# Moving the last gelu into the PSUM evacuation, and the closing spatial pass's partial sum from TensorE to VectorE

## The chip, the cores and the metric

The kernel runs on one core of one Trainium2 chip. The metric is the device time of one execution in microseconds (us). Executions of one kernel spread by several us (the kernel before: 1929.6 to 1937.5), so times here are medians of three to seven executions. Readings inside a run (stage lengths, idle times) come from one profiled execution each. Engines: PE is TensorE (PEld its weight loads), ACT is ScalarE, DVE is VectorE, POOL is GpSimd, SP issues most DMAs. PSUM holds the products that PE writes (`ps_all` in the profiles), SBUF the other tiles. The granted clock is the share of its full clock that TensorE got, by the profile. An "exp" is one instruction of the softmax on ACT, from PSUM to the tile `Pa`.

## The reference, cut to what matters

```python
x = A_x                                        # 1 x 2048 x 512, bf16
for layer in (0, 1):                           # the same weights twice
    n = layernorm(x)
    x = x + attention(n)                       # 32 query heads of 16, one key/value head
    n = layernorm(x)
    z = gelu_tanh(n @ w_in)                    # 2048 x 1792
    z1, z2 = z[:, :896], layernorm(z[:, 896:])
    g = w_sp @ z2 + b_sp                       # "spatial": mixes tokens
    x = x + (z1 * g) @ w_out
```

The spatial product needs z2 of all 2048 tokens, and layer 1's attention needs keys of all tokens of x. So each layer ends with work that few exps can cover.

## The kernel before: the parts that matter

The kernel contains its own planner. Every operation is given a modelled duration, dependencies and a priority. The planner plays the program through with these numbers, and the order in which operations are taken becomes each engine's fixed program order. An operation may list alternative engines (`alts`).

Attention goes in chunks of 512, 512, 512, 256, 128 and 128 tokens. After each chunk its tokens pass through the mixer's first half. The spatial product is done in four passes over the source tiles: 0 to 7, 8 to 11, 12 and 13 (partial sums in fp16 in `gp`), and the closing pass over tiles 14 and 15. `tc` counts eight pairs of target token tiles.

```python
# mixer_chunk, for every chunk: copy out of PSUM (DVE, or ACT as alternative), then gelu in place on ACT
def gl(e):
    e.activation(z1v[:, :, 0:n], z1v[:, :, 0:n], ACTF.Gelu_apprx_tanh)
    return e.activation(z2f[...], z2f[...], ACTF.Gelu_apprx_tanh)
ge = sc.op("act", gl, ..., z1 + z2, -1.0, table="gelu")
...                                   # bn_stats of z2 on DVE after ge, rstd on POOL, normalise on DVE

# spatial(..., final=True), for each tc: 4 PSUM jobs of up to 2 x 256 columns
if final:
    todo.append(("g", None))          # partial sum through an fp16 identity, on PE
todo += [("w", w) for w in ws]        # the two source tiles
...
fn=lambda e, b, ...: e.tensor_tensor(self.hT[...], PSUM, z1r[...], ALU.mult)    # DVE, from PSUM
...                                   # then 2 x 7 output products of 512 columns on PE, priority pr - 0.3,
                                      # and X = PSUM + X on DVE for each of the two tiles
```

`hT` has two buffers, used by turns. Layer 0's closing pass also builds layer 1's keys, pair by pair.

The softmax here doesn't subtract the row's maximum and nothing guards it: scores larger than these inputs give would overflow.

## Time and profile before

1933.8 us, median of three runs (1931.3 to 1937.45). I mark two times in every profile: the end of layer 0's last exp (T0) and the end of layer 1's last exp (T1).

| before | us |
|---|---|
| T0 | 905.2 |
| T0 to T1 (layer 0's end, then layer 1's attention) | 956.7 |
| T1 to the end of the span (layer 1's end) | 71.3 |
| exp work done in the first 200 us after T0 | 124.9 |
| ACT idle from T0 + 200 to T1 | 24.2 |

The view of the exps' line gives 126.2 for the fourth row, since it counts with them a table load of 1.28 us at the same line (timeline, ACT):

```profile
954.28 1.28 ACT L1257 ACT_TABLE_LOAD   x1
```

Over the whole span the busy line of the page has ACT at 90% and DVE at 92%, but at the layers' ends another engine rules. The windows view of the kernel before, three stretches of 10 us from T0 (columns: window, length, busy time and count of PE, PEld, DVE, ACT and POOL, granted clock, DMA share, GB/s):

```profile
905.20:915.20 10.00, 9.30 (x91) 6.87 (x91) 9.95 (x22) 0.60 (x1) 0.77 (x2) 1.00 0.01 2
915.20:925.20 10.00, 7.60 (x75) 5.90 (x74) 8.71 (x17) 5.85 (x8) 0.00 (x0) 1.00 0.07 20
925.20:935.20 10.00, 8.05 (x39) 4.89 (x40) 4.75 (x10) 0.00 (x0) 0.78 (x2) 0.66 0.18 49
```

PE falls idle, and in the third stretch the granted clock is 0.66. The timeline of PE shows why (start, length, engine, line, operation, shapes, count, and in brackets the idle time before it with its releaser):

```profile
919.56 3.44 PE L1034 MATMUL ps_all<-wsT,z2n 128*128 128x256 bf16 x30
927.15 0.40 PE L1032 MATMUL ps_all<-gp,ident_3 128*128 128x256 f16 x1 [4.15 <-DVE z2n L943]
927.34 0.63 PE L1034 MATMUL ps_all<-z2n 128*128 128x256 bf16 x2
```

The closing pass waits 4.15 us for the last chunk's normalised z2 and then runs slowly. In layer 1 the same chunk goes through these steps (timeline, ACT and DVE):

```profile
1877.36 1.28 ACT L921 ACT_TABLE_LOAD   x1
1878.66 0.95 ACT L921 ACTIVATE E<-E 128x896 bf16<-128x896 bf16 x1
1879.51 0.93 ACT L922 ACTIVATE z2n<-z2n 128x896 bf16<-128x896 bf16 x1
...
1880.84 1.14 DVE L934 BATCH_NORM_STATS2 st_18<-z2n 128x6 f32<-128x448 bf16 x2
```

In the last stage PE never rests. The chain of waits (start, length, what):

```profile
1889.46 3.02 PE ps_all L1087 x14
1892.48 0.22 PE ps_all L1034 x2
1892.70 0.11 PE ps_all L1032
...
1894.78 3.02 PE ps_all L1087 x14
```

A pair of token tiles takes 1894.78 - 1889.46 = 5.32 us, of which L1032, the identity product, takes 7 x 0.11.

### The profile page before, as it was taken

How to read it: one execution, taken by the hardware profiler on the slowest of the kernel's cores; microseconds unless marked ns; L12 is line 12 of the kernel's file. 1: busy time of each engine (PE TensorE's matmuls, PEld its weight loads, DVE VectorE, ACT ScalarE, POOL GpSimd, SP SyncE). 2: the span in 40 equal slices, each digit the busy share in tenths (PEclk: the TensorE clock that was granted, in tenths of full speed). 3: DMA queues.
4: the chain of work that ended last, by engine and by line, in shares of the span. 5: the costliest groups of instructions: out<-in, count | busy, mean ns of one | idle time of the engine just before them, and what ended most of it. 6: DMA issues, size and time to landing. Idle time of an engine off the chain costs nothing.

```text
span 1933.2 us, 41389 instructions
## 1 busy us (share of the span) xinstructions
PE 1649.2 (85%) x17431; PEld 671.0 (35%) x17431; DVE 1777.4 (92%) x3198; ACT 1747.3 (90%) x1526; POOL 59.7 (3%) x106
## 2 busy tenths in 40 slices
PE   6777887787989998889987877877788999888899
PEld 3222222122234443555542222222122444335565
DVE  7999999999998898987769999989999899999976
ACT  7999999999999999997379999999999999999960
POOL 3000000000000000000000000000000000000000
PEclk9999999999999999999999999999998999989999
DMA  9700001000001000112100000010000100010123
GB/s 262 191 1 1 1 1 42 1 1 1 1 31 34 23 8 26 46 28 62 53 10 1 1 1 1 1 42 1 1 1 20 34 23 23 2 53 8 29 71 101
DMA packets 96985, 59.84 MB, mean 31 GB/s; under 512 B 39704, under 2 KB 92704, under 8 KB 96800
## 3 DMA queue, kind: packets, MB, share of 16 engines
q1 hardware_dynamic: 95216, 56.64, 10.6%
q8 instruction: 138, 2.26, 0.5%
q10 hardware_dynamic: 1584, 0.56, 0.1%
q14 instruction: 47, 0.39, 0.1%
HBM read 30.97 MB, written 17.83 MB: 25 GB/s over the span
## 4 chain that ended last, share of the span: by engine, by line
ACT 32%; PE 30%; DVE 25%; issue 12%; POOL 1%; ACTq 0%; POOLq 0%
ACT Pa L1257 29%; PE ps_all L1034 8%; PE ps_all L1540 7%; DVE E L1437 5%; PE ps_all L1333 4%; DVE Pd L1475 4%; PE ps_all L1087 3%; DVE E L1473 2%; DVE E L1464 2%; DVE E L1470 2%; DVE gp L1050 2%; PE ps_all L1523 1%; PE ps_all L748 1%; DVE E L1467 1%; ACT z2n L922 1%
## 5 line engine op out<-in xcount | busy, mean ns | idle before, releaser
L1257 ACT ACTIVATE Pa<-ps_all 128x1536 bf16<-128x1536 f32 (+1 forms) x1435 | 1640.0, 1349 | 59.6 <-PE ps_all L1540 46.0
L1540 PE MATMUL ps_all<-qs,kT 32*128 32x512 bf16 (+2 forms) x6144 | 572.8, 315 | 227.9 <-ACT Pa L1257 213.9
L1540 PEld LDWEIGHTS ps_all<-qs,kT 32*128 32x128 bf16 x6144 | 172.6, 92 | 710.1 <-ACT Pa L1257 631.0
L1437 DVE TENSOR_SCALAR E<-ps_all 128x512 int32<-128x512 f32 x510 | 347.9, 685 | 26.8 <-PE ps_all L1540 24.0
L1333 PE MATMUL ps_all<-Pa,V 128*32 128x512 bf16 (+2 forms) x5407 | 331.4, 316 | 2.0 <-DVE oT L771 1.5
L1475 DVE SCALAR_TENSOR_TENSOR Pd<-E 128x1024 uint16<-128x1024 int32 x255 | 310.2, 1217 | 0.8
L1523 PE MATMUL ps_all<-wo_r,zero 128*128 128x512 bf16 (+2 forms) x967 | 257.2, 369 | 2.2 <-DVE E L1437 1.8
L1034 PE MATMUL ps_all<-wsT,z2n 128*128 128x256 bf16 x1456 | 216.8, 276 | 4.7 <-DVE gp L1050 2.9
L1333 PE MATMUL ps_all<-Pd,V 128*32 128x512 bf16 (+2 forms) x737 | 181.0, 324 | 0.0
L1470 DVE TENSOR_TENSOR E<-E 128x1024 f16<-128x1024 f16 x255 | 174.8, 685 | 3.2
L1473 DVE TENSOR_TENSOR E<-E 128x1024 f16<-128x1024 f16 x255 | 174.4, 684 | 2.1
L1464 DVE TENSOR_SCALAR E<-E 128x1024 f16<-128x1024 uint16 x255 | 174.6, 686 | 1.1
L1034 PEld LDWEIGHTS ps_all<-wsT,z2n 128*128 128x128 bf16 x1456 | 119.5, 98 | 72.3 <-issue 36.3
L1333 PEld LDWEIGHTS ps_all<-Pa,V 128*32 128x32 bf16 x5407 | 98.7, 96 | 120.9 <-issue 99.6
L1523 PEld LDWEIGHTS ps_all<-wo_r,zero 128*128 128x128 bf16 x967 | 74.4, 100 | 122.0 <-issue 90.5
L1467 DVE TENSOR_SCALAR E<-E 128x1024 f16<-128x1024 f16 x255 | 106.9, 419 | 2.5
L1466 DVE TENSOR_SCALAR E<-E 128x1024 f16<-128x1024 f16 x255 | 107.0, 420 | 2.2
L1050 DVE TENSOR_TENSOR gp<-ps_all,gp 128x512 f16<-128x512 f32 (+1 forms) x128 | 75.3, 616 | 16.6 <-PE ps_all L1034 16.4
L748 PE MATMUL ps_all<-xnTA,wq_pad 128*128 128x512 bf16 (+2 forms) x384 | 68.8, 312 | 2.7 <-DVE E L1437 2.3
L876 PE MATMUL ps_all<-w_in_r,xnTB 128*128 128x448 bf16 x256 | 64.6, 361 | 1.3 <-DVE z2n L885 0.6
L902 PE MATMUL ps_all<-xnTB,w_in_r 128*128 128x512 bf16 (+2 forms) x336 | 63.0, 310 | 1.7 <-DVE z1s L911 1.4
L771 DVE CAST oT<-ps_all 128x512 bf16<-128x512 f32 (+2 forms) x96 | 48.7, 508 | 7.8 <-PE ps_all L1333 7.3
(79 smaller groups left out, 1168.5 us busy)
## 6 DMA issues: line engine op xcount, KB each, us to landing
wsT<-wsT_scratch SPq DMA_DIRECT2D x18, 512.0 KB, 3.9
wsT_scratch<-gp SPq DMA_DIRECT2D x16, 512.0 KB, 3.7
z1s<-z_scratch SPq DMA_DIRECT2D x16, 448.0 KB, 3.7
z_scratch<-z1s SPq DMA_DIRECT2D x6, 896.0 KB, 4.5
wsT<-wsT_scratch SPq DMA_DIRECT2D x16, 256.0 KB, 2.9
X<-in_A_x_dram SPq DMA_DIRECT2D x8, 256.0 KB, 6.4
z2n<-wsT_scratch SPq DMA_DIRECT2D x2, 1024.0 KB, 7.6
out_dram<-X SPq DMA_DIRECT2D x16, 128.0 KB, 1.7
```

Of the source, the lines that this page charges most:

```text
L1034: ins = e.matmul(o_, self.z2n[:, w[0], f * 128:(f + 1) * 128], w[1], start=st, stop=sp_)
L1050: return e.tensor_tensor(dst, src, dst, ALU.add)
L1257: return e.activation(k.Pa[:, base:base + n, :], k.b32(b0, n).rearrange("p (k q) -> p k q", k=n), ACTF.Exp, scale=SCALE)
L1333: ins = e.matmul(k.b32(k.pvb)[32 * j:32 * j + 32, 0:n], k.V[:, kt, 32 * j:32 * j + 32], b.slot[:, s * n:(s + 1) * n], tile_position=(0, 32 ...
L1437: return k.sc.op("dve", lambda e: e.tensor_scalar(k.eI[:, s, 512 * i:512 * (i + 1)], k.b32(j.bank.idx)[:, 0:512], C_LOG2, C_BIAS, op0=ALU. ...
L1464: return lambda e: e.tensor_scalar(out, a, m, None, op0=ALU.mult)
L1467: return lambda e: e.tensor_scalar(out, a, m, b, op0=ALU.mult, op1=ALU.add)
L1470: o4 = sc.op("dve", lambda e: e.tensor_tensor(q, u, w, ALU.mult), d_sb(n, 0.521e-3), [o3], pr)
L1473: o6 = sc.op("dve", lambda e: e.tensor_tensor(q, q, u, ALU.mult), d_sb(n, 0.521e-3), [o5], pr)
L1475: o7 = sc.op("dve", lambda e: e.scalar_tensor_tensor(po.bitcast(U16), I, 2.0 ** -9, q, op0=ALU.mult, op1=ALU.add), d_sb(n, 1.042e-3), [o6] ...
L1523: ins = e.matmul(k.b32(k.pvb if b is None else b.idx)[:, 0:n], k.zero[:], k.wo_r[:, 0, 0:n], start=b is not None, stop=b is not None)
L1540: ins = e.matmul(self.b32(bank)[:, s * n:(s + 1) * n], self.kT[32 * j:32 * j + 32, kt * 128:(kt + 1) * 128], self.qs[32 * j:32 * j + 32, g ...
```

## The change

Its intent: take 56 identity products per layer off PE, by adding the partial sum on DVE from SBUF, where an fp16 add of 1024 columns took 0.685 us in this profile, as long as a multiply of 512 from PSUM (0.682), and by letting the idle ACT empty PSUM. And bring the last chunk's z2 sooner, by doing the gelu while emptying PSUM, with its table loaded ahead. The core of the diff:

```diff
+GPL = 0                      # identity product only in layers below GPL: nowhere
+MERGE = 9                    # merging of two chunks: never, there are six
@@ mixer_chunk
+con = dict(fn=lambda e, b, cp=cp: e.activation(*cp(b), ACTF.Gelu_apprx_tanh), eng="act", table="gelu", ...)
-   [dict(fn=lambda e, b, cp=cp: e.tensor_copy(*cp(b)), ...)]
+   [con] if last else [dict(fn=lambda e, b, cp=cp: e.tensor_copy(*cp(b)), ...)]
+if last:
+    gs = z2
+    pre = sc.op("act", lambda e: e.activation(self.tiny[:], self.mhalf[:], ACTF.Exp), ..., table="exp")
@@ spatial
-if final:
+if gp_pe:                    # gp_pe = final and layer < GPL
     todo.append(("g", None))
-fn=lambda e, b, ...: e.tensor_tensor(self.hT[...], PSUM, z1r[...], ALU.mult)
+h16 = h_.bitcast(FP16)       # h_ is the slice of hT
+fn=lambda e, b, cp=cp: e.tensor_copy(*cp(b)), dur=d_psum(256 * m), prio=1.1, deps=self.hT_read[par],
+alts=[("act", lambda e, b, cp=cp: e.activation(*cp(b), ACTF.Copy), d_act(256 * m))]
+ad = sc.op("dve", ... tensor_tensor(h16, h16, self.gp[:, tc, f0:f0 + m, :], ALU.add) ...)
+ev = sc.op("dve", ... tensor_tensor(h_, h16, z1r[:, par, f0:f0 + m, :], ALU.mult) ...)
@@ ExpStream.commit, after a layer's last exp
+k.sc.op("act", lambda e: e.activation(k.tiny[:], k.mhalf[:], ACTF.Gelu_apprx_tanh), ..., table="gelu")
# cut: the rewriting of the loads of the third pass, which with these constants gives the same loads
```

More of the change, by code (lines that the diff above doesn't have):

```diff
@@ L289, in job @@
             o = self.op(c.get("eng", "dve"), (lambda en, f=c["fn"]: f(en, j.bank.idx)), c["dur"],
-                        [prev] + outs[-1:] + list(c.get("deps", ())), c["prio"], job=j, alts=alts)
+                        [prev] + outs[-1:] + list(c.get("deps", ())), c["prio"], job=j, alts=alts,
+                        table=c.get("table"))
             outs.append(o)
@@ L418, in __init__ @@
         self.s_fin = 14
+        self.merge = MERGE
         self.ring = [(0, 3), (3, 2)]
@@ L431, in __init__ @@
         self.mhalf = sb([P, 1], FP32, "mhalf")
+        self.tiny = sb([P, 1], FP32, "tiny")
         self.X = sb([P, self.NT, D], BF16, "X")
@@ L882, in cp @@
                     return self.z2n[:, t, h * 448:(h + 1) * 448], self.b32(b)[:, 0:448]
+                con = dict(fn=lambda e, b, cp=cp: e.activation(*cp(b), ACTF.Gelu_apprx_tanh), eng="act", table="gelu",
+                           dur=d_act(448), prio=pr - 1, deps=list(self.z2_read.get(t, ())))
                 pl, (ev,) = sc.job([((lambda e, b, pe=pe: pe(e, b, (0, 1))), 2 * d_mm(448)),
                                     ((lambda e, b, pe=pe: pe(e, b, (2, 3))), 2 * d_mm(448))],
-                                   [dict(fn=lambda e, b, cp=cp: e.tensor_copy(*cp(b)), dur=d_psum(448), prio=pr - 1,
+                                   [con] if last else [dict(fn=lambda e, b, cp=cp: e.tensor_copy(*cp(b)), dur=d_psum(448), prio=pr - 1,
                                          deps=list(self.z2_read.get(t, ())),
@@ L891, in mixer_chunk @@
                 self.xnTB_read.append(pl)
-        z1v = self.z1L if last else self.z1s[:].rearrange("p (f t) -> p f t", f=NF)
+        c0 = g.t0 % 512 if g.ci == self.merge + 1 else 0
+        z1v = (self.z1L if last else self.z1s[:].rearrange("p (f t) -> p f t", f=NF))[:, :, c0:c0 + n]
         z1_war = list(self.dx_s.end) if last else list(self.z1s_free)
@@ L906, in cp @@
             def cp(b, f0=f0, m=len(fs)):
-                return (z1v[:, f0:f0 + m, 0:n], self.b32(b)[:, 0:m * n].rearrange("p (f t) -> p f t", f=m))
+                return (z1v[:, f0:f0 + m, :], self.b32(b)[:, 0:m * n].rearrange("p (f t) -> p f t", f=m))
             w = max(2, 1024 // n)
+            con = dict(fn=lambda e, b, cp=cp: e.activation(*cp(b), ACTF.Gelu_apprx_tanh), eng="act", table="gelu",
+                       dur=d_act(n * len(fs)), prio=pr - 0.9, deps=z1_war)
             pl, (ev,) = sc.job([((lambda e, b, part=mm[i:i + w], pe=pe: pe(e, b, part)), len(mm[i:i + w]) * d_mm(n))
                                 for i in range(0, len(mm), w)],
-                               [dict(fn=lambda e, b, cp=cp: e.tensor_copy(*cp(b)), dur=d_psum(n * len(fs)), prio=pr - 1,
+                               [con] if last else [dict(fn=lambda e, b, cp=cp: e.tensor_copy(*cp(b)), dur=d_psum(n * len(fs)), prio=pr - 1,
                                      deps=z1_war,
@@ L917, in mixer_chunk @@
             self.xnTB_read.append(pl)
+        if g.ci == self.merge:
+            self.held = (T, z1, z2)
+            return
+        t0 = T[0]
+        if g.ci == self.merge + 1:
+            T, z1, z2 = [a + b for a, b in zip(self.held, (T, z1, z2))]
+            t0, T = T[0], T
+            z1v = self.z1s[:].rearrange("p (f t) -> p f t", f=NF)[:, :, 0:128 * len(T)]
+        nt = len(T)
         z2f = self.z2n[:].rearrange("p t f -> p (t f)")
         def gl(e):
-            e.activation(z1v[:, :, 0:n], z1v[:, :, 0:n], ACTF.Gelu_apprx_tanh)
-            return e.activation(z2f[:, T[0] * FH:(T[0] + nt) * FH], z2f[:, T[0] * FH:(T[0] + nt) * FH],
-                                ACTF.Gelu_apprx_tanh)
-        ge = sc.op("act", gl, d_act(NF * n) + d_act(nt * FH), z1 + z2, -1.0, table="gelu")
-        sp = self.dma(lambda e: e.dma_start(self.z1_dv[:, :, g.t0:g.t0 + n], z1v[:, :, 0:n]), [ge],
-                      f"z1s{g.layer}{g.ci}", n * P * NF * 2)
+            e.activation(z1v, z1v, ACTF.Gelu_apprx_tanh)
+            return e.activation(z2f[:, t0 * FH:(t0 + nt) * FH], z2f[:, t0 * FH:(t0 + nt) * FH], ACTF.Gelu_apprx_tanh)
+        if last:
+            gs = z2
+            pre = sc.op("act", lambda e: e.activation(self.tiny[:], self.mhalf[:], ACTF.Exp), 0.1, z1 + z2, 2.0, table="exp")
+        else:
+            gs = z1 = [sc.op("act", gl, d_act(NF * nt * 128) + d_act(nt * FH), z1 + z2, -1.0, table="gelu")] * (2 * nt)
+        sp = self.dma(lambda e: e.dma_start(self.z1_dv[:, :, t0 * 128:(t0 + nt) * 128], z1v), z1,
+                      f"z1s{g.layer}{g.ci}", nt * P * P * NF * 2)
         if last:
@@ L930, in mixer_chunk @@
             self.z1s_free = [sp]
-        self.z1_spill.append((g.t0, g.t0 + n, sp))
+        self.z1_spill.append((t0 * 128, (t0 + nt) * 128, sp))
         ag = []
@@ L934, in mixer_chunk @@
             s_ = [sc.op("dve", lambda e, t=t, h=h: e.bn_stats(self.st2[:, t, h, :], self.z2n[:, t, h * 448:(h + 1) * 448]),
-                        0.53, [ge], pr - 0.3) for h in range(2)]
+                        0.53, [gs[2 * (t - t0) + h]], pr - 0.3) for h in range(2)]
             ag.append(sc.op("dve", lambda e, t=t: e.bn_aggr(self.mv2[:, t, :], self.st2[:, t, :, :]), 0.13, s_, pr - 0.4))
@@ L971, in spatial @@
         nst = s1 - s0
+        early = not final and nst < 4
+        gp_pe = final and layer < GPL
         z2f = self.z2n[:].rearrange("p t f -> p (t f)")
-        if nst == 2 and not final:
+        if early:
+            slot0 = self.wsT[:, 0:8, :].rearrange("p s t -> p (s t)")
             self.wsP = []
-            self.wsP_ld = []
-            for h in range(2):
-                w_ = z2f[:, 4096:6144] if h == 0 else self.wsT[:, 0:8, :].rearrange("p s t -> p (s t)")
-                w_ = w_.rearrange("p (s t) -> p s t", s=2)
-                war = [o for t in (4, 5, 6) for o in self.z2_read[t]] if h == 0 else self.last_ws[0]
-                self.wsP.append(w_)
-                self.wsP_ld.append(self.dma(lambda e, h=h, w_=w_: e.dma_start(
-                    w_, self.ws_dv[:, s0:s1, 1024 * h:1024 * (h + 1)]), war + self.ws_st[s0:s1], f"wsp{h}", 524288, 1.0))
-            self.wsF = z2f[:, 0:4096].rearrange("p (s t) -> p s t", s=2)
+            nf = self.NT - s1
+            parts = [(0, 4, z2f[:, 2048:5120], (2, 3, 4, 5)), (4, 6, z2f[:, 5120:6656], (5, 6, 7)),
+                     (6, 8, slot0[:, 0:1536], None)]
+            if nst == 2:
+                parts = [(0, 4, z2f[:, 4096:6144], (4, 5, 6)), (4, 8, slot0, None)]
+            for (c0, c1, w_, tiles) in parts:
+                w_ = w_.rearrange("p (s t) -> p s t", s=nst)
+                war = self.last_ws[0] if tiles is None else [o for t in tiles for o in self.z2_read[t]]
+                ld = self.dma(lambda e, w_=w_, c0=c0, c1=c1: e.dma_start(w_, self.ws_dv[:, s0:s1, 256 * c0:256 * c1]),
+                              war + self.ws_st[s0:s1], f"wsp{c0}", (c1 - c0) * nst * 65536, 1.0)
+                for tc in range(c0, c1):
+                    self.wsP.append((w_[:, :, 256 * (tc - c0):256 * (tc - c0 + 1)], ld, tiles))
+            self.held_f = range(0, 3 if nf == 1 else 5)
+            self.wsF = z2f[:, 0:2048 * nf].rearrange("p (s t) -> p s t", s=nf)
             self.wsF_ld = self.dma(lambda e: e.dma_start(self.wsF, self.ws_dv[:, s1:self.NT, :]),
-                                   [o for t in range(5) for o in self.z2_read[t]] + self.ws_st[s1:], "wsf", 1048576, 1.5)
+                                   [o for t in self.held_f for o in self.z2_read[t]] + self.ws_st[s1:], "wsf", nf * 524288, 1.5)
         for tc in range(8):
@@ L990, in spatial @@
                 ws = [(s, self.wsF[:, s - s0, tc * 256:(tc + 1) * 256]) for s in range(s0, s1)]
-            elif nst == 2:
-                h, c = tc // 4, tc % 4 * 256
-                lds = [self.wsP_ld[h]]
-                ws = [(s, self.wsP[h][:, s - s0, c:c + 256]) for s in range(s0, s1)]
+                held = self.held_f
+            elif early:
+                w_, ld, held = self.wsP[tc]
+                lds = [ld]
+                ws = [(s, w_[:, s - s0, :]) for s in range(s0, s1)]
             else:
@@ L1001, in spatial @@
                 lds = [ld]
+                held = ()
                 ws = [(s, self.wsT[:, 8 * sl + s - s0, :]) for s in range(s0, s1)]
@@ L1041, in spatial @@
                     deps.append(self.l_b)
-                if final:
+                if gp_pe:
                     deps += [self.c_id16] + [self.gp_ops[(tc, f)] for f in fs]
                 m = len(fs)
-                if not final:
+                if gp_pe:
+                    pl, (ev,) = sc.job(pieces, [dict(
+                        fn=lambda e, b, par=par, f0=f0, m=m: e.tensor_tensor(
+                            self.hT[:, par, f0:f0 + m, :], self.b32(b)[:, 0:256 * m].rearrange("p (f t) -> p f t", f=m),
+                            z1r[:, par, f0:f0 + m, :], ALU.mult),
+                        dur=d_psum(256 * m), prio=0.9, deps=[zld] + self.hT_read[par])], deps, pr)
+                    hs.append(ev)
+                    ad = pl
+                elif not final:
                     def ev_fn(e, b, tc=tc, f0=f0, m=m):
@@ L1059, in spatial, with cp @@
                 else:
+                    h_ = self.hT[:, par, f0:f0 + m, :]
+                    h16 = h_.bitcast(FP16)
+                    def cp(b, h16=h16, m=m):
+                        return h16, self.b32(b)[:, 0:256 * m].rearrange("p (f t) -> p f t", f=m)
                     pl, (ev,) = sc.job(pieces, [dict(
-                        fn=lambda e, b, par=par, f0=f0, m=m: e.tensor_tensor(
-                            self.hT[:, par, f0:f0 + m, :], self.b32(b)[:, 0:256 * m].rearrange("p (f t) -> p f t", f=m),
-                            z1r[:, par, f0:f0 + m, :], ALU.mult),
-                        dur=d_psum(256 * m), prio=0.9, deps=[zld] + self.hT_read[par])], deps, pr)
+                        fn=lambda e, b, cp=cp: e.tensor_copy(*cp(b)), dur=d_psum(256 * m), prio=1.1, deps=self.hT_read[par],
+                        alts=[("act", lambda e, b, cp=cp: e.activation(*cp(b), ACTF.Copy), d_act(256 * m))])], deps, pr)
+                    ad = sc.op("dve", lambda e, h16=h16, tc=tc, f0=f0, m=m: e.tensor_tensor(
+                        h16, h16, self.gp[:, tc, f0:f0 + m, :], ALU.add), d_sb(256 * m, 0.521e-3),
+                        [ev] + [self.gp_ops[(tc, f)] for f in fs], 0.9)
+                    ev = sc.op("dve", lambda e, h_=h_, h16=h16, par=par, f0=f0, m=m: e.tensor_tensor(
+                        h_, h16, z1r[:, par, f0:f0 + m, :], ALU.mult), d_sb(256 * m, 0.521e-3), [ad, zld], 0.9)
                     hs.append(ev)
@@ L1067, in spatial @@
                     for f in fs:
-                        self.gp_read[(tc, f)] = [pl]
+                        self.gp_read[(tc, f)] = [ad]
                 users.append(pl)
@@ L1071, in spatial @@
                     self.z2_read[s].append(pl)
-                for s in range(0, 5) if final else (range(4, 7) if nst == 2 and tc < 4 else ()):
+                for s in held or ():
                     self.z2_read[s].append(pl)
-            if nst > 2:
+            if not final and not early:
                 self.last_ws[sl] = [users[-1]]
-            elif not final and tc > 3:
+            elif held is None:
                 self.last_ws[0] = [users[-1]]
@@ L1271, in commit @@
             k.sc.lend(r, range(b0, b0 + k.ring[r][1]), o)
+            if not self.queue:
+                k.sc.op("act", lambda e: e.activation(k.tiny[:], k.mhalf[:], ACTF.Gelu_apprx_tanh), 0.1, [o, k.c_mh], -2.0,
+                        table="gelu")
 class PVStream:
```

## The prediction

> **What bounds the kernel now.** In most of each layer ScalarE's exp does (busy line: ACT 90%, DVE 92%, PE 85% of 1933.2 us). The change touches only the two stages without a full stream of exps: layer 0's end (905 to 1006 us) and layer 1's end (1862 to 1933). There PE is the limit (windows view): busy 26.9 of 27 us from 927 to 954, 48.3 of 52 from 954 to 1006, 39.75 of 39.75 from 1885.25 to 1925. By the chain of waits each pair of token tiles in the last stage takes 5.31 us: 3.02 us of output product and 2.29 us for 21 matmuls of 256 columns, 0.109 us each; 7 of these only add the fp16 partial sum through an identity.
>
> **What the change does.** GPL=0 and MERGE=9 mean (from the code) that the identity product goes in both layers and chunks are never merged; the "early" loads equal the old ones. What remains:
> 1. 56 identity matmuls go in each layer: 56 x 0.109 = 6.1 us of PE.
> 2. Per pair, 4 multiplies from PSUM on DVE (3 x 0.68 + 0.42 = 2.5 us) become 4 copies to fp16 (ACT: 0.60 us at 512 columns, 0.38 at 256, in all 2.2 us; on DVE when exps are queued), 4 fp16 adds and 4 multiplies from SBUF. An fp16 add of 1024 columns takes 0.685 us here; I estimate 0.36 at 512, 0.23 at 256, so 1.3 us for adds and 1.3 for multiplies. With two residual adds DVE goes from 3.9 to 4.0 us per pair, under PE's new 4.55. The Trainium skill, "VectorE: DVE Perf Modes" (tier table), gives tensor_tensor twice the rate on 16-bit SBUF operands, single rate from PSUM; the trace agrees (0.67 against 1.34 ns per column).
> 3. The last chunk's copies, table load (1.28 us) and two gelus (0.95, 0.93) become gelus in the evacuation, with the table loaded earlier. The statistics, at 923.8 and 1880.8 us, start some 4.5 us sooner.
>
> **How much is on the path.** Layer 0's end: PE idles 4.15 us before the closing pass (to 927.15), then runs at half rate to 932 (0.21 us per matmul, granted clock 0.76 in 920 to 930), about 2.4 us lost; "TensorE: Matmul & The Clock Gate" (Part 1) states that an idle window drops the clock, as this trace shows. Potential: 6.1 + 4.1 + 2.4 = 12.6 us. Against it: a longer chain per pair (copy, add, multiply: about 0.7 us more), copies among restarting exps, and waits on DVE that PE has already. I take 8. Layer 1's end: 6.1 plus about 2 us of PE idle before 1885, less 1 for the longer chain and DVE's backlog of partial sums (10 of 10 us busy in 1880 to 1890): 7.
>
> **Prediction: 1934 - 15 = 1919 us** (0.8% faster), 1910 to 1928 eight times in ten. Faster by over 2%: 0.03; within 2%: 0.96; slower by over 2%: 0.01.
>
> **What would show it.** Right: last-stage pairs at 4.5 to 4.7 us; PE idle before layer 0's closing pass under 1.5 us and no low clock after it; ACT doing most copies; exp at full rate near 998 us. Wrong: pairs over 5 us with PE waiting for DVE's multiply, or the exp restart not earlier.
>
> **What would make it wrong.** Copies landing on DVE (0.69 us each); adds or multiplies not at the double rate; the static order, computed from other durations, putting a DVE operation ahead of one that PE needs; a shifted order in layer 1's long attention stage, a few us either way.

## The result, and the profile after

The changed kernel: 1918.4 us, median of four runs (1915.4 to 1920.2). The ratio to before is 0.9913, with a 95% interval of 0.989 to 0.9936. (A ratio here is the mean time of one kernel's runs over that of the other's of the same rounds, so not quite the ratio of the medians.) In these rounds the kernel before took 1935.6 us (median of four). The prediction of 1919 us holds.

T0 itself is no result: all kernels here have the same program up to about there, and yet it fell between 900.0 and 907.4 us in the profiles. So I compare stretches that start at T0 or T1.

| | before | after |
|---|---|---|
| T0 to T1 | 956.7 | 950.8 |
| exp work in the first 200 us after T0 | 124.9 | 138.2 |
| ACT idle from T0 + 200 to T1 | 24.2 | 29.2 |
| T1 to the end | 71.3 | 62.0 |

Windows of the changed kernel, from its T0 (903.13):

```profile
903.13:913.13 10.00, 9.31 (x91) 6.86 (x91) 9.95 (x22) 2.08 (x3) 0.77 (x2) 1.00 0.01 2
913.13:923.13 10.00, 9.80 (x97) 8.02 (x97) 9.95 (x22) 6.63 (x13) 0.79 (x2) 1.00 0.09 25
923.13:933.13 10.00, 9.35 (x59) 5.45 (x58) 9.91 (x28) 3.17 (x7) 0.61 (x2) 1.00 0.32 92
```

PE's hole and the low clock are gone. The gelu of layer 1's last chunk (timeline, ACT and DVE):

```profile
1866.41 0.54 ACT L888 ACTIVATE z2n<-ps_all 128x448 bf16<-128x448 f32 x1 [1.30 <-PE ps_all L881]
1867.16 0.54 ACT L888 ACTIVATE z2n<-ps_all 128x448 bf16<-128x448 f32 x1 [0.21 <-PE ps_all L881]
1867.59 1.14 DVE L956 BATCH_NORM_STATS2 st_19<-z2n 128x6 f32<-128x448 bf16 x2
```

The statistics start while the second half is still being evacuated, 13.7 us after T1; before it was 18.9. But the last stage is not what I foretold. Its timeline on PE (L1066 is the spatial product, L1135 the output product):

```profile
1882.29 2.78 PE L1066 MATMUL ps_all<-z2n 128*128 128x256 bf16 x24
1886.19 6.22 PE L1135 MATMUL ps_all<-E 128*128 128x512 bf16 x28 [1.12 <-DVE E L1111]
1892.24 3.22 PE L1066 MATMUL ps_all<-z2n 128*128 128x256 bf16 x28
1896.48 3.19 PE L1135 MATMUL ps_all<-E 128*128 128x512 bf16 x14 [1.01 <-DVE E L1111]
```

Two pairs take 1896.48 - 1886.19 = 10.29 us, 5.15 us each: 0.17 us better than before, where I had 4.5 to 4.7. PE does two pairs' output products in a row (28), then two pairs' spatial products (28), and then waits for DVE's multiply (L1111). So the 9.3 us won after T1 had to come from elsewhere, and at the other end 13.3 us more of exps in 200 us became only 5.9 us by T1. These two questions are what the experiments are for.

### The profile page after: what moved, and what is told of

Read it like the earlier page. It is cut to its first block, busy times and chain, and to the rows that moved or that the text cites. A ratio compares the mean times of both kernels' runs of the same rounds, so it can differ in the third digit from the quotient of the medians.

```text
span 1915.9 us, 41287 instructions
## 1 busy us (share of the span) xinstructions
PE 1633.4 (85%) x17316; PEld 656.5 (34%) x17316; DVE 1783.8 (93%) x3276; ACT 1770.5 (92%) x1576; POOL 60.5 (3%) x106
## 4 chain that ended last, share of the span: by engine, by line
ACT 35%; PE 28%; DVE 24%; issue 12%; POOL 1%; ACTq 0%; DVEq 0%; POOLq 0%
ACT Pa L1305 32%; PE ps_all L1591 8%; PE ps_all L1066 6%; PE ps_all L1384 4%; DVE E L1488 4%; DVE Pd L1526 3%; PE ps_all L1135 2%; DVE E L1521 2%; DVE E L1524 2%; DVE gp L1090 2%; DVE E L1515 2%; PE ps_all L1574 2%; ACT z2n L941 1%; DVE st_15 L602 1%; PE ps_all L753 1%
## 5 line engine op out<-in xcount | busy, mean ns | idle before, releaser
L1066 PE MATMUL ps_all<-wsT,z2n 128*128 128x256 bf16 x1456 | 218.1, 276 | 5.5 <-DVE gp L1090 3.8
L1066 PEld LDWEIGHTS ps_all<-wsT,z2n 128*128 128x128 bf16 x1456 | 119.0, 98 | 75.1 <-issue 37.3
L1574 PEld LDWEIGHTS ps_all<-wo_r,zero 128*128 128x128 bf16 x964 | 73.4, 100 | 124.1 <-issue 92.5
L1090 DVE TENSOR_TENSOR gp<-ps_all,gp 128x512 f16<-128x512 f32 (+1 forms) x128 | 75.4, 614 | 13.3 <-PE ps_all L1066 13.2
L1135 PE MATMUL ps_all<-E 128*128 128x512 bf16 x224 | 52.1, 380 | 6.3 <-DVE E L1111 5.6
```

The source lines that it names most:

```text
L1066: ins = e.matmul(o_, self.z2n[:, w[0], f * 128:(f + 1) * 128], w[1], start=st, stop=sp_)
L1090: return e.tensor_tensor(dst, src, dst, ALU.add)
L1574: ins = e.matmul(k.b32(k.pvb if b is None else b.idx)[:, 0:n], k.zero[:], k.wo_r[:, 0, 0:n], start=b is not None, stop=b is not None)
```

## The experiments

All outputs are right. "Before" in the same rounds was 1932 to 1934 us.

### Each part alone

`e1_gelu_only` puts the identity product back in both layers, `e2_pass_only` puts the old gelu back, `e3_identity_in_layer0` puts the identity back in layer 0 only.

```diff
-GPL = 0
+GPL = 2                                 # e1; e3 has GPL = 1
```
```diff
-   [con] if last else [dict(            # e2, in two places
+   [dict(
-        if last:
+        if False:
             gs = z2
-            if not self.queue:          # the early gelu table
+            if False:
```

> The changed kernel with the identity products back in both layers (GPL = 2), so only the last chunk's gelu from PSUM and the early table loads are new. Theory A (my prediction's split: dropped identity products carry 12 us, the sooner gelu 2 us of layer 1's end and the idle and low clock of layer 0's end): time near 1928 us, layer 1's end (last exp to the end of the span) 69 us against 71.3 before. Theory B (the sooner gelu carries most, because it lets the closing pass start 5 us earlier, and the identity products' saving is mostly given back as PE waits): time near 1924 us, layer 1's end near 65.5 us; closing pass still 5.3 us per pair.

> The changed kernel with the last chunk's old gelu (copy, table load, two gelus) and no early table loads; only the closing pass is new. Theory A: time near 1926 us, layer 1's end near 66 us. Theory B: time near 1930 us, layer 1's end near 68 us, with output products of two pairs in a row on PE and a PE wait for VectorE's multiply after them.

> Identity products back in layer 0 only (GPL = 1). Layer 1's end should stay as in the changed kernel, 62 us, under both theories. Theory A: the 6.1 us of PE come back in layer 0, time near 1924 us. Theory B (part of a sooner exp restart is lost later as ScalarE idle, whatever gave it): time 1919 to 1921 us, though fewer exps are done in the 200 us after layer 0's last exp than the changed kernel's 138 us.

| | time | ratio (95%) | T0 to T1 | exps in 200 us | full rate after T0 | T1 to end |
|---|---|---|---|---|---|---|
| before | 1933.9 | | 956.7 | 124.9 | 100.3 | 71.3 |
| e1 gelu only | 1928.2 | 0.997 (0.9949 to 0.9991) | 955.9 | 125.7 | 99.9 | 66.1 |
| e2 pass only | 1941.9 | 1.005 (1.0035 to 1.0065) | 964.9 | 130.2 | 95.4 | 73.4 |
| e3 identity in layer 0 | 1925.9 | 0.9965 (0.9948 to 0.9982) | 955.9 | 125.7 | 99.9 | 62.8 |
| after | 1918.4 | 0.9913 (0.989 to 0.9936) | 950.8 | 138.2 | 87.3 | 62.0 |

"Full rate" is when the first unbroken row of exps starts, counted from T0. The timeline of ACT gives it, here for before, e1 and after, whose T0 are 905.20, 907.25 and 903.13 (each followed by exps without a gap):

```profile
1005.54 2.36 ACT L1257 ACTIVATE Pa<-ps_all 128x1024 bf16<-128x1024 f32 x2 [0.18 <-PE ps_all L1540]
```
```profile
991.94 3.71 ACT L1305 ACTIVATE Pa<-ps_all 128x1536 bf16<-128x1536 f32 x3 [0.18 <-PE ps_all L1591]
1002.81 1.02 ACT L635 ACTIVATE xnTA<-ps_all 128x1024 bf16<-128x1024 bf16 x1 [7.16 <-PE ps_all L626]
...
1007.19 5.54 ACT L1305 ACTIVATE Pa<-ps_all 128x1024 bf16<-128x1024 f32 x5 [0.71 <-PE ps_all L1591]
```
```profile
990.41 6.90 ACT L1305 ACTIVATE Pa<-ps_all 128x1024 bf16<-128x1024 f32 x6 [0.45 <-PE ps_all L1591]
```

The parts do not add up. Alone they gave -5.7 and +8.1 us against the median of these rounds; together they had given -15. The pass alone even made the kernel slower, though it had 5.3 us more of exps done in the first 200 us. The gelu alone healed the clock in layer 0 and still brought full rate no sooner: its exps started sooner but then ACT stood 7.16 us, waiting at last for the transposed tokens from which the last pair's keys are made. Why those keys came no sooner I leave open. Of the theories, A hit e1's time (1928) but not its end (69 against 66.1), and B its end (65.5) but not its time (1924). For e2 both missed both: they had 1926 to 1930 us and an end of 66 to 68. For e3 the end came near the 62 that both had, and the time of 1925.9 is nearer to A (1924) than to B (1919 to 1921). But in these runs the whole order of layer 1 was planned anew, so its end began from different states. The next square mends that.

### A square for layer 1's end, from one state

Four kernels whose programs are the same up to T1: both parts (the changed kernel), and each or both undone in layer 1 only.

```diff
-    [con] if last else [dict(                                    # a1 and a3: old gelu in layer 1
+    [con] if last and g.layer == 0 else [dict(
-        if last:
+        if last and g.layer == 0:
             gs = z2
-            if not self.queue:
+            if not self.queue and blocks[0].unit.grp.layer == 0:
-        gp_pe = final and layer < GPL                            # a2 and a3: identity product in layer 1
+        gp_pe = final and layer == 1
```

> The changed kernel with the last chunk's gelu of layer 1 done the old way; its program is the changed kernel's up to layer 1's last exp, so only layer 1's end (62.0 us in the changed kernel) may differ. It is one of a square of four (neither, gelu only, pass only, both = the changed kernel) that start from the same state. Additive theory: neither near 71, gelu only near 66, pass only near 67, both 62. Rival (the closing pass pays only after the sooner gelu, as the run of the pass alone suggested): pass only no shorter than neither. This run: 67 us under the first, 71 or more under the rival.

> The changed kernel with the identity products back in layer 1 only, same program up to layer 1's last exp. Gelu only: layer 1's end near 66 us under both theories, with 5.3 us per pair in the last stage. If the dropped identity products gave their full 6.1 us, it would be 68.

> The changed kernel with both parts undone in layer 1 only, same program up to layer 1's last exp. Layer 1's end near 71 us, as before the change (71.3), if the state at the last exp does not matter to it; some microseconds off if it does (how many partial sums of the third pass are still to be done then).

| layer 1 has | T1 to end | time |
|---|---|---|
| neither (a3) | 70.8 | 1929.4 |
| gelu only (a2) | 65.5 | 1925.0 |
| pass only (a1) | 67.1 | 1923.3 |
| both (after) | 62.0 | 1918.4 |

From one state the parts add up within 0.2 us: the gelu is worth 5.3 (5.1 with the pass), the pass 3.7 (3.5 with the gelu). The rival falls: that the pass alone looked harmful at this end was the state it began from. e2 had 181 matmuls of the third pass left at T1, these four kernels have 104. Why the gelu is worth 5 us, where I had allowed some 2, shows in PE's timeline of a1, then of the changed kernel:

```profile
1877.04 4.90 PE L1066 MATMUL ps_all<-z2n 128*128 128x256 bf16 x28 [3.83 <-DVE z2n L965]
```
```profile
1871.58 3.23 PE L1066 MATMUL ps_all<-z2n 128*128 128x256 bf16 x28
```

Without the sooner gelu the third pass ends before z2 is there: PE stands 3.83 us and the 28 products then take 4.90 us in place of 3.23. This is the same as in layer 0 of the kernel before. It is not the shorter closing pass that opens the hole, for a3, with the old pass, shows it too (timeline, PE):

```profile
1879.56 0.28 PE L1064 MATMUL ps_all<-gp,ident 128*128 128x256 f16 x1 [3.83 <-DVE z2n L965]
```

The state at T1 does: in layer 1 of the kernel before 152 matmuls of the third pass were left, and they filled that hole, which is why I saw only about 2 us of it.

### Why the pass gives 3.6 us and not 6.1

My theory: PE's output products of two pairs come in a row because their priority is higher, and so the longer chain (copy, add, multiply) of the next two pairs is left uncovered. The rival: DVE, with two more operations per job, is now the limit. First try, in both layers, then in layer 1 alone from the same state:

```diff
-    ..., hs + [self.l_wout], pr - 0.3)
+    ..., hs + [self.l_wout], pr + 0.3)                             # e5
+    ..., hs + [self.l_wout], pr + (0.3 if layer else -0.3))        # a4
```

> The changed kernel with one priority altered: in the closing pass the spatial products go before the output products (pr + 0.3 in place of pr - 0.3), so PE's program alternates 14 and 14 matmuls by pair rather than 28 and 28. If PE's waits in layer 1's closing pass (0.33 + 1.12 + 1.01 + 1.11 us and some smaller) come from this order: layer 1's end 58 to 60 us in place of 62, about 4.6 us per pair, time near 1914 us. Rival (VectorE's added work is the limit there): layer 1's end stays within 1 us of 62, time 1917 to 1920.

> The changed kernel with the spatial products of the closing pass ahead of the output products in layer 1 only (pr + 0.3 there), same program up to layer 1's last exp, where the first such run had changed the whole order of layer 1. If PE's four waits of about 1 us in the changed kernel's last stage come from two output products in a row: layer 1's end 58 to 60 us, time near 1915 us, PE periods of 4.55 us per pair. Rival (VectorE's added work limits the last stage): 61 to 63 us.

e5 took 1916.5 us, T0 to T1 950.4, T1 to the end 64.1: the expectation was missed. It planned layer 1 anew and left partial sums of the third pass for the last stage, where DVE was hardly idle until its last multiply (57.3 us busy after T1, against 52.5 in the changed kernel). It doesn't decide; PE still waited 2.13 us for DVE's last multiplies there. a4 does: T1 to the end is 58.6 us, time 1914.7. PE's timeline of a4 (one matmul record of some groups is missing in the trace):

```profile
1884.83 1.69 PE L1066 MATMUL ps_all<-z2n 128*128 128x256 bf16 x14
1886.58 2.97 PE L1135 MATMUL ps_all<-E 128*128 128x512 bf16 x13
1889.38 1.69 PE L1066 MATMUL ps_all<-z2n 128*128 128x256 bf16 x14
1890.91 3.19 PE L1135 MATMUL ps_all<-E 128*128 128x512 bf16 x14
1893.93 1.69 PE L1066 MATMUL ps_all<-z2n 128*128 128x256 bf16 x14
```

A pair now takes 1889.38 - 1884.83 = 4.55 us, exactly the estimate of the prediction, and these pairs have no wait between them. So from this state the order took the other 3.3 us, not DVE's speed: against a2 the pass is now worth 65.5 - 58.6 = 6.9 us. (The old pass was not run with the other priority. PE's waits in a2's closing pass are 1.6 us in all, so it had little to gain.) The waits view, PE's waits in the closing pass, changed kernel and then a4, says the same (us in total, times, longest):

```profile
PE ps_all L1135 <- DVE E L1111: 3.6, 4, 1.1
```
```profile
PE ps_all L1135 <- DVE E L1111: 0.8, 2, 0.6
```

### Where half of the gain at layer 0's end went

After its first 200 us the changed kernel has 13.3 us more of exps behind it. The windows view of ACT from there to T1 (its busy time is the fourth), before and after:

```profile
1105.20:1861.93 756.73, 649.48 (x7321) 257.02 (x7321) 709.61 (x1269) 732.53 (x631) 17.33 (x26) 0.98 0.06 17
```
```profile
1103.13:1853.93 750.80, 644.76 (x7277) 256.82 (x7275) 699.10 (x1253) 721.56 (x620) 18.43 (x26) 0.98 0.07 20
```

ACT is busy 11.0 us less (the exps as a whole took 2 us longer in this profile), but it idles 5.0 us more (29.2 against 24.2) and so reaches T1 only 5.9 us sooner. Five profiles of this order gave 950.1 to 954.9 us, so the 5.9 is known only to a few us, but the timed runs agree: of some 15 us in all, 9 are won after T1. So about 5 us were given back as idle time of ACT in layer 1's attention, which the change does not touch, and e2 gave back 13. Either the change harms it (S), or the fixed order planned for it is better or worse by luck (L). The test is a nudge that asks the chip for the same work: one modelled duration, 0.03 us longer, in layer 1 only.

```diff
-        ev = sc.op("dve", lambda e: e.tensor_copy(self.oT[...], ...), d_psum(n),
+        ev = sc.op("dve", lambda e: e.tensor_copy(self.oT[...], ...), d_psum(n) + 0.03 * g.layer,
```

The value was the first one taken, but I had seen the planner's own forecast for it before the runs. So the size of the gain is no fair sample of what nudges do.

> The kernel before, with 0.03 us added to one duration in its planning (the copy that ends a head group, in layer 1 only). The chip is asked for the same work; only the order of layer 1's attention is planned anew. Question: what lengthens layer 1's attention by some 6 us in the changed kernel (ScalarE idle 29 to 32 us after its first 200 us against 24 before) and by 13 in the run of the pass alone. Theory L (luck of the planned order): with this nudge the time from layer 0's last exp to layer 1's (956.7) moves by more than 3 us either way while the exps done in the first 200 us stay at 126. Rival S (the change itself slows the later attention): it stays at 955 to 958.

> The run of the closing pass alone (1942 us, last exp to last exp 964.9 us, 131.5 us of exps in the first 200) with the same nudge. Theory L: last exp to last exp falls to 951 to 958, time near 1930 us, with the first 200 us unchanged within 2 us. Rival S: it stays above 962.

> The changed kernel with the same nudge. Theory L: last exp to last exp leaves the range of the five runs of the changed kernel's order (950.1 to 954.9 us), either way, with 138 us of exps in the first 200 as before; if the 12 us won there are kept, 944 to 948. Rival S: it stays in 950 to 955.

> A version that may beat both: the changed kernel with the nudge and with the spatial products first in layer 1's closing pass. Last exp to last exp as in the nudged changed kernel, within 3 us; layer 1's end 58 to 62 us, since the nudged order may leave more partial sums of the third pass for it. Near 1910 us if the nudge does no harm.

| | time | T0 to T1 | exps in 200 us | ACT idle after | T1 to end |
|---|---|---|---|---|---|
| before, nudged | 1927.6 (1932.4 in the same rounds) | 951.2 (956.7) | 124.3 (124.9) | 17.6 (24.2) | 71.1 (71.3) |
| pass only, nudged | 1925.6 (1941.9) | 949.7 (964.9) | 129.2 (130.2) | 20.8 (37.0) | 70.6 (73.4) |
| after, nudged | 1905.6 (1918.4) | 935.2 (950.8) | 138.2 (138.2) | 15.6 (29.2) | 63.4 (62.0) |
| after, nudged, spatial first in layer 1 | 1905.9 | 935.2 | 138.2 | 15.6 | 62.7 |

The windows view from T0 + 200 to T1 of the nudged changed kernel, to compare with the one above:

```profile
1106.15:1841.33 735.18, 627.93 (x7172) 252.64 (x7222) 687.57 (x1238) 719.59 (x619) 16.25 (x26) 0.97 0.07 19
```

ACT does the same work within 2 us, in 15.6 us less. And the waits view, ACT's exps waiting for the score products in those windows, changed kernel and then nudged:

```profile
ACT Pa L1305 <- PE ps_all L1591: 23.2, 47, 2.2
```
```profile
ACT Pa L1305 <- PE ps_all L1591: 13.5, 32, 0.9
```

Rival S falls and theory L fits: all three moved, with the exps of the first 200 us unchanged within 1 us, and with the nudge ACT idles no longer in the changed kernel (15.6) than in the kernel before (17.6). Both nudged forms of the new pass moved further than their expectations had said (951 to 958, and 944 to 948 at best). Three limits belong to this. Profiles of one unchanged order already spread over 4.8 us, so the 5.5 us of the first row rest on the timed runs (ratio to before 0.9972, 0.9957 to 0.9988). All three moved the same way under the one value that was tried, so luck in each order isn't told from a nudge that suits the planner in general. And in e2 the granted clock from T0 + 200 to T1 was 0.96, against 0.98 with the nudge; whether that is a cause of its loss or a result is not shown (the changed kernel won its 15.6 us at 0.97 against 0.98).

The pass alone, which had looked like a loss of 8 us, is a gain of about 7 on the kernel before with another order (1925.6, ratio 0.9965), though only 2 us better than the kernel before with the same nudge. The nudged changed kernel beats both kernels: ratio 0.9859 (0.9844 to 0.9873). With the same nudge on both sides, the change is worth 1927.6 - 1905.6 = 22 us. What it gains where it acts is near that: 11.0 us less for ACT to do and 8.8 at layer 1's end, 19.8. So the measured 15 us probably understates it, but one pair of orders is no average. Putting the spatial products first on top of the nudge added nothing beyond noise (1905.9), and its end of 62.7 just missed the 58 to 62 expected. PE's waits in the middle of the last stage went, but it stood 2.13 us for DVE's last multiplies.

The experiments show that the planned order can move the time by as much as the change does. They don't show which operations stand wrongly in it. That is left open.

## Why the prediction was right, point by point

- **The total** (1919 foretold, 1918.4 measured) was right, but two of its terms were mis-sized against each other, and a third loss that I had named only as "a few us either way" took the rest. That they met within 1 us of 1919 was partly luck: the profiles have 5.9 us won up to T1 and 9.3 after it, where I had 8 and 7.
- **Layer 1's end**, "6.1 plus about 2 us of PE idle before 1885, less 1", 7 in all: it brought 8.8 (70.8 to 62.0). Both sources were right, and the split was wrong. The dropped identity products brought 3.6 and not 5; the sooner gelu brought 5.2 and not 2. For the first, "last-stage pairs at 4.5 to 4.7 us" failed: it was 5.15, with PE waiting for DVE's multiply. This is the prediction's own sign of being wrong ("pairs over 5 us with PE waiting for DVE's multiply"), and it named, under what would make it wrong, "the static order ... putting a DVE operation ahead of one that PE needs". The runs showed the order at work, on PE itself: two output products in a row. With another priority the pair took 4.55, as estimated. For the second, I had read the idle time that existed. In the new order, with fewer matmuls of the third pass left at T1, the same late z2 would have cost 3.83 us of idle and 1.7 us of slow matmuls.
- **Layer 0's end**, "Potential: 12.6 us ... I take 8": 13.3 us arrived as exps done sooner, and left ACT 11.0 us less to do. I had expected a loss on the spot, from the longer chain. There was none to speak of; about 5 us were lost later instead, as idle time of ACT in the attention of layer 1, where the nudges point to its planned order. "Exp at full rate near 998 us" was 92.8 after T0; it came 87.3 after T0.
- **PE's hole and the clock in layer 0**: right. The Trainium skill, "TensorE: Matmul & The Clock Gate" (Part 1), says that an idle window brings the clock to half. The trace agrees: after 4.15 us idle the 256-column products took 0.21 us each in place of 0.109, and after 3.83 us idle 28 of them took 4.90 us in place of 3.23. After the change the granted clock in this stretch is 1.00.
- **Costs of the moved work**: right. In a row, DVE's adds and multiplies from SBUF start 0.335 us apart at 512 columns and 0.202 at 256, which is 0.52 ns for each further column. The old multiplies from PSUM start 0.598 and 0.331 us apart, 1.04 ns for each further column. This is the halving that the Trainium skill, "VectorE: DVE Perf Modes" (the perf-mode tier table), gives. ACT did 57 of the 64 copies, 0.60 us each at 512 columns.

## What to carry to other kernels

Take work from the bottleneck engine only after asking what will then wait: the shorter closing pass gave its full worth only in an order that kept PE fed, and what a late input cost depended on how much other work was left to cover it. In a statically planned kernel, measure a change at the place where it acts (work done by a fixed time, the length of a stage from one common state), because the order planned for everything after it may give or take as much as the change itself. Before judging a part by the total, plan it again with nudges that change nothing else, more than one if you can.

## What the Trainium skill lacked or had wrong

- "ScalarE: Activation LUTs" (What ACT_TABLE_LOAD costs) gives about 1283 ns for the load plus about 1380 ns of drain, 2.66 us in all. The load took 1.28 us here as stated, but no drain shows: in the kernel before the copy ahead of it ended at 1877.34, the load ran from 1877.36, and the gelu started 0.01 us after its end. All its 24 loads but the first look like this (at most 0.08 us idle before them, 0.01 after).
- No page that I read warns how much a statically planned program depends on its order ("Perfetto Trace Analysis" would be a place for it): 0.03 us added to one modelled duration moved layer 1's attention from 950.8 to 935.2 us with ACT's work the same within 2 us.
